# Three row splits and three transposes of a wide unit, moved one unit earlier

## The chip, the cores and the metric

One core of a Trainium2 chip runs the whole kernel. The time is the device time of one execution in microseconds; the number shown for a kernel is the median over several executions.

## The reference

The inputs are q, k and v of 4 batches, 12 heads, 448 positions and 64 columns. The reference computes attention with normalised q and k, and lays the result out as x of 1792 rows and 768 columns. Two mixture layers follow, each with 8 experts:

```
e_idx = argmax(logits of the row)
for e in range(8):
    h = max(x[rows of e] @ w1[e], 0)        # 768 -> 1024
    out[rows of e] = gate[rows of e] * (h @ w2[e])   # 1024 -> 768
```

The first layer has one more gate factor, and the second adds a bias to its logits that depends on a modality number. Each row goes to one expert only, so the rows have to be gathered by expert, multiplied with that expert's two matrices, and scattered back. Everything is in float32.

## The kernel before

**Units.** The work of the two mixture layers is cut into units. A unit is up to 304 rows of one expert: they are gathered from memory into `xr` (three tiles of 128, 128 and 48 rows), multiplied with `w1` (the first product, 8 output blocks, steps 0 to 7) and with `w2` (the second product, 6 output blocks, steps 8 to 13), and scattered to the output. Every float32 operand is split into a float16 high part and a bfloat16 low part, and a product takes three matmuls per pair of 128 by 128 blocks (line 378). The high part is a cast on ScalarE, and the low part a subtraction on VectorE or GpSimd (lines 310 and 311 for weights, 361 and 362 for rows).

**The order of units.** The second layer ends with six units, `seq`: three wide units of up to 304 rows (j = 0, 1, 2), a narrow remainder unit of up to 64 rows (j = 3), a wide unit (j = 4), and a second narrow one (j = 5). The change concerns `seq[4]`, the wide unit between the two remainder units. Below, W2 is `seq[2]`, R3 is `seq[3]`, W4 is `seq[4]`, and R5 is `seq[5]`. A narrow unit has its own planes for rows and for second-layer weights (`XTx`, `wxh`, `wxl`); W2 and W4 share the planes `XT`.

**Preparing a unit's rows.** For a unit, four steps run ahead of its first matmul: its table of rows `pay` is loaded (SyncE, line 345); from this VectorE computes row numbers `idx` (line 352) and GpSimd gathers the rows (line 357); each tile is split (lines 361 and 362) into `XS`; and each tile of `XS` is turned by a DMA transpose into `XT`, issued from SyncE (line 365).

**Where these steps are placed.** `M.unit` calls `do(s)` behind step s. There `XPLAN[late]` gives splits and transposes of the next unit, and `side` gives extra functions by step. `do(0)` also loads `pay` of the unit after the next one, and `do(7)` computes its `idx` and gathers it. Before the change, W2 carries the splits of W4 as `side` functions behind its steps 11, 12 and 13, and R3 carries the three transposes behind its step 1 (`XPLAN[6]`).

**Queues.** Every engine works in the order in which it is given instructions. SyncE issues the weight loads, the loads of `pay`, and the transposes, all on one DMA queue. Around the change its order is: `w1` block 0 and 1 of W4 (tile `r`), then block 2, block 3, block 4 and 5, `pay` of R5, the three transposes, then eight loads of `w2` of W4 (tiles `raw`, `r2a` and `r2b`). The blocks of `r` wait for their six buffers, which the split of R3's `w1` frees one by one. The split of W4's `w1` runs during R3's second product: casts on ScalarE (`w1h`), subtractions on VectorE (`w1l`).

Of the kernel before, what the change touches and what calls it, by code (L numbers as in the profile page):

```python
# [27 lines left out]
class Moe:  # L28
# [366 lines left out]
    def unit(self,u,nx=None,fx=None,side=None,late=0,mid=None,fast={},now=False,fp=0,fr=7,**kw):  # L395

        gen=self.gen(); side=dict(side or {})
        plan=XPLAN[late] if nx is not None else {}
        def do(s):
            if fx is not None and s==fp: self.fetch_pay(fx)  # L400
            for k,t in plan.get(s,()):
                if t<nx.ntl:
                    if k=="t": self.xtrans(nx,t)
                    else: self.xsplit(nx,t,self.nc.gpsimd if k=="p" else None)
            if fx is not None and s==fr: self.fetch_rows(fx)
            for _ in range(fast.get(s,1)): next(gen,None)
            for f in side.pop(s,()): f()
# [90 lines left out]
        yield  # L498
        yield from self.route_g(sp,sm,l,ntl,R,nx["ohsum"],nx["ord"],iv=iv,pay=pay,tag="tp",lag=True)

XPLAN={5:{1:[("s",1),("t",0)],2:[("s",2),("t",1)],3:[("t",2)]},7:{9:[("s",0),("t",0)]},4:{0:[("p",0)],2:[("t",0),("t",1),("t",2)]},6:{1:[("t",0),("t",1),("t",2)]},0:{0:[("p",0),("p",1),("p",2)],7.5:[("t",0),("t",1),("t",2)]},3:{3:[("s",0)],4:[("s",1)],5:[("s",2)],7.5:[("t",0),("t",1),("t",2)]},
1:{8:[("s",0),("s",1),("s",2),("t",0),("t",1),("t",2)]},
    2:{7.5:[("s",0),("s",1),("s",2),("t",0),("t",1),("t",2)]},None:{10:[("s",0),("t",0)]}}
class LazyUnit:
# [329 lines left out]
def body_full(tc,q,k,v,g_q,g_k,wg,wog,w1,w2,mod,wg2,bias2,v1,v2,out,stop=False,O=None):  # L834
    nc=tc.nc
    with ExitStack() as ctx:
        M=Moe(tc,ctx)
# [120 lines left out]
        def stepper(name):  # L958
            def f():
                if name not in S: S[name]=F[name]()  # L960
                next(S[name],None)
            return f
# [18 lines left out]
        sides={1:{KF+j:[stepper("table1")] for j in range(6)},2:{7:[stepper("pick2")]*2,**{j:[stepper("pick2")] for j in range(8,14)}},3:{7:[stepper("pick3")]*2,**{j:[stepper("pick3")] for j in range(8,14)}}}  # L981
# [21 lines left out]
        seq=S["B"][:3]+[S["S"][0],S["B"][3],S["S"][1]]  # L1003
# [8 lines left out]
        def load(t,n): return nc.values_load(t[0:1,0:1],min_val=0,max_val=n)  # L1012
        def chain(n,i,m,unit):
            if i>=m: return
            with tc.If(n>i):
                u=unit(i); cold(u); M.unit(u); M.flush()
                chain(n,i+1,m,unit)
        def others(u,nx,fx):
            def f(done):
                sl,tn=M.slot,M.turn  # L1020
                assert M.post is None
                with tc.If(S["over"]>0):  # L1022
                    ent,ni=S["s1"]
                    chain(load(ni,G1),0,G1,lambda i: Unit(L1,ent,i,128))
                    c=lp.tile([128,E],F32,name="c4"); M.reduce_counts(tp,c2,lp,tag="tp",out=c)
                    rem=lp.tile([128,E],F32,name="rem"); nc.vector.tensor_tensor(out=rem,in0=c,in1=off2,op=ALU.subtract)
                    for _ in M.chunks(S["b4"],lp,M.nchunks(lp,rem,N2,0),off2,c,N2,G4): pass
                    be4,n4=S["b4"]
                    chain(load(n4,G4),0,G4,lambda i: Unit(L2,be4,i,N2))
                    M.redo(u,nx,fx,tn,done)  # L1030
                M.slot,M.turn=sl,tn; u.e=None
                if nx is not None: nx.e=None
            return f
        def known(): S["over"]=load(over,E+G2+G1)
        def px(t): return lambda: M.xsplit(seq[4],t,nc.gpsimd)
        sides={0:{0:[more],3:[known]},2:{KF+3+t:[px(t)] for t in range(3)},4:{KF+1:[nc.gpsimd.drain]}}
        for u in seq: u.own=True
        for j,u in enumerate(seq):
            nx,fx=seq[j+1] if j<5 else None,seq[j+2] if j<4 else None
            M.unit(u,nx=nx,fx=fx,side=sides.get(j),late={2:4,3:6,4:4}.get(j,0),mid=others(u,nx,fx) if j==0 else None)  # L1040
        M.flush()
        pin(tc,mark)

# [28 lines left out]
```

## Time and profile before

| what | value |
|---|---|
| time, median of 3 runs | 881.64 us (878.62 to 884.17) |
| profiled execution | 877.29 us, span 875.6 us |
| mean granted clock of TensorE | 0.98 |
| busy share: TensorE matmul, VectorE, ScalarE, GpSimd | 93%, 74%, 62%, 45% |

The rows below have times in microseconds from the start of the span of the profiled execution. PE is TensorE's matmuls, PEld its weight loads, DVE is VectorE, ACT is ScalarE, POOL is GpSimd and SPq is SyncE's issuing of DMAs. A name such as L365 is the line that issued the instruction, `XT<-XS` says that it writes XT and reads XS. A bracket at a row's end gives how long the engine stood idle before it and what ended that.

### The profile page before, as it was taken

To read this page: it belongs to the slowest core of one execution; us is meant where nothing else is said; L and a number is where in the kernel's file an instruction comes from. 1 tells how busy PE (TensorE), PEld (TensorE's weight loads), DVE (VectorE), ACT (ScalarE), POOL (GpSimd) and SP (SyncE) were. 2 spreads that over 40 slices of the span, in tenths; PEclk is the share of its full clock that TensorE was granted. 3 is DMA by queue.
4 is the path that set the end of the run, shared out by engine and by line. 5 is a ranking of instruction groups with operands and counts; after the bars stand their busy time and mean duration, and the time that the engine had idled before them with its cause. 6 is when DMAs were issued, how large, how long until landed. Compare 5 with 4: busy or idle time off the path is not lost. (4 is left out here: it accounts for less than half of the span.)

```text
span 875.6 us, 23286 instructions
## 1 busy us (share of the span) xinstructions
PE 817.9 (93%) x8881; PEld 640.0 (73%) x8898; DVE 649.3 (74%) x1302; ACT 545.0 (62%) x1039; POOL 389.9 (45%) x397
## 2 busy tenths in 40 slices
PE   4698999998998899899999999999999999999897
PEld 1265666665665588777889999988677768878676
DVE  6689889888778775786797767776676846577674
ACT  4577777776776654655556686776545535456563
POOL 5677777876776623131424333344402524024301
PEclk9799999998999989999999999999999999999999
DMA  5567665766465482979486797898677759896961
GB/s 137 130 152 183 162 155 162 201 161 163 114 172 142 143 229 77 278 290 326 105 321 145 275 320 201 249 348 239 204 251 280 235 108 332 192 315 207 291 245 52
DMA packets 142137, 181.42 MB, mean 207 GB/s; under 512 B 71944, under 2 KB 109592, under 8 KB 142016
## 3 DMA queue, kind: packets, MB, share of 16 engines
q1 hardware_dynamic: 134048, 157.06, 62.9%
q0 software_dynamic: 6656, 22.32, 7.8%
q8 instruction: 71, 1.16, 0.6%
q10 hardware_dynamic: 1312, 0.47, 0.2%
q14 instruction: 50, 0.41, 0.2%
HBM read 129.73 MB, written 23.94 MB: 176 GB/s over the span
## 5 line engine op out<-in xcount | busy, mean ns | idle before, releaser
L378 PE MATMUL pl<-XT,w1h 128*128 128x304 f16 (+6 forms) x1236 | 210.5, 275 | 4.9 <-PEq L1022 2.0
L378 PE MATMUL pl<-hh,w2h 128*128 128x304 f16 (+7 forms) x720 | 194.4, 275 | 0.0
L378 PE MATMUL pl<-hh,w2l 128*128 128x304 f16 (+7 forms) x720 | 194.1, 274 | 0.0
L378 PE MATMUL pl<-hl,w2h 128*128 128x0 bf16 x720 | 187.9, 264 | 3.0 <-DVE hl L382 3.0
L378 PE MATMUL pl<-XT,w1l 128*128 128x304 f16 (+6 forms) x618 | 172.5, 279 | 0.0
L680 POOL TENSOR_TENSOR plo<-p 128x448 f16<-128x448 f32 x142 | 140.3, 1005 | 56.1 <-ACT p L677 52.4
L378 PEld LDWEIGHTS <-w1h 128*128 128x128 f16 x1536 | 134.5, 98 | 27.4 <-ACTq L1022 2.3
L378 PEld LDWEIGHTS <-w2h 128*128 128x128 f16 x1440 | 134.0, 98 | 24.6 <-issue 1.4
L311 DVE TENSOR_TENSOR w1l<-r,w1h 128x1024 bf16<-128x1024 f32 x90 | 109.7, 1233 | 46.5 <-ACT w1h L310 46.5
L456 ACT COPY yt<-pl 128x304 f32<-128x304 f32 (+8 forms) x102 | 36.6, 358 | 117.2 <-PE pl L378 117.2
L362 POOL TENSOR_TENSOR XS<-xr,XS 128x768 bf16<-128x768 f32 (+5 forms) x27 | 46.8, 1749 | 130.4 <-ACT XS L361 100.6
L381 ACT ACTIVATE hh<-pl 128x304 f16<-128x304 f32 (+8 forms) x135 | 49.1, 364 | 81.0 <-PE pl L378 69.5
L677 ACT ACTIVATE p<-pst,eb 128x896 f32<-128x896 f32 (+1 forms) x96 | 86.5, 911 | 14.8 <-PE pst L673 13.9
L310 ACT CAST w1h<-r 128x1024 f16<-128x1024 f32 x90 | 93.5, 1056 | 0.1
L690 PE MATMUL av<-vv,p 128*128 128x65 f16 (+1 forms) x768 | 89.8, 199 | 1.8 <-ACT xrow L702 1.8
L690 PEld LDWEIGHTS <-p 128*128 128x128 bf16 (+1 forms) x768 | 73.5, 102 | 20.8 <-issue 15.0
L692 PE MATMUL av<-vv,plo 128*128 128x65 f16 (+1 forms) x768 | 88.0, 196 | 0.6 <-DVE plo L680 0.6
L691 PE MATMUL av<-vv,p 128*128 128x64 f16 (+1 forms) x768 | 88.5, 198 | 0.0
L654 DVE TENSOR_REDUCE m<-psm 128x2 f16<-128x896 f32 x70 | 76.0, 1086 | 9.1 <-PE psm L649 7.3
L378 PEld LDWEIGHTS <-w1l 128*128 128x128 bf16 x768 | 74.1, 98 | 11.8
L378 PEld LDWEIGHTS <-w2l 128*128 128x128 bf16 x720 | 70.3, 98 | 16.7 <-issue 4.1
L382 DVE SCALAR_TENSOR_TENSOR hl<-pl,hh 128x304 bf16<-128x304 f32 (+8 forms) x135 | 53.5, 398 | 34.8 <-ACT hh L381 34.4
(328 smaller groups left out, 1806.3 us busy)
## 6 DMA issues: line engine op xcount, KB each, us to landing
r<-in_moe_w_dram SPq DMA_DIRECT2D x96, 512.0 KB, 8.9
raw<-in_moe_w_dram SPq DMA_DIRECT2D x64, 384.0 KB, 5.9
r2a<-in_moe_w_dram SPq DMA_DIRECT2D x32, 384.0 KB, 6.8
r2b<-in_moe_w_dram SPq DMA_DIRECT2D x32, 384.0 KB, 8.9
T<-Z SPq DMA_DIRECT2D x48, 224.0 KB, 3.8
T<-Z SPq DMA_DIRECT2D x48, 112.0 KB, 2.9
yd<-zero SPq DMA_DIRECT2D x14, 384.0 KB, 3.1
rv<-in_v_dram SPq DMA_DIRECT2D x24, 192.0 KB, 4.2
```

The lines of the kernel that those rows point to most:

```text
L310: if part!=1: nc.scalar.copy(h,t)
L311: if part!=0: (eng or nc.vector).tensor_tensor(out=l,in0=t,in1=h,op=ALU.subtract)
L362: if part!=0: (eng or nc.vector).tensor_tensor(out=self.XS[:m,t,1].bitcast(BF16),in0=x,in1=h,op=ALU.subtract)
L378: self.nc.tensor.matmul(o,a,b,start=i==0,stop=i==tot-1); i+=1
L381: nc.scalar.activation(h,p,AF.Relu)
L382: nc.vector.scalar_tensor_tensor(out=l,in0=p,scalar=0.0,in1=h,op0=ALU.max,op1=ALU.subtract)
L654: if t<3: nc.vector.tensor_reduce(m[:,t:t+4:3],p[:,:,:S],axis=AX.X,op=ALU.max,negate=True)
L677: self.nc.scalar.activation(self.d["P",i][:,self.u(kt)],p[:,:nn,:S],AF.Exp,bias=self.eb,scale=0.125)
L680: eng.tensor_tensor(out=self.d["L",i][:,u],in0=P[:,u],in1=self.hi(P)[:,u],op=ALU.subtract)
L690: nc.tensor.matmul(o,hh,w[:,0:65],start=kt==0,stop=False)
L691: nc.tensor.matmul(o[:,0:64],hh,w[:,65:129],start=False,stop=False)
L692: nc.tensor.matmul(o,ll,w[:,0:65],start=False,stop=kt==3)
```

## The change

The splits of W4's rows move from behind steps 11, 12 and 13 of W2 to behind its steps 10, 11 and 12. The transposes move from behind step 1 of R3 to behind steps 11, 12 and 13 of W2, each one step behind its split. R3's plan for its next unit is then empty (`XPLAN[8]`).

```
-6:{1:[("t",0),("t",1),("t",2)]}
+8:{}
...
         def px(t): return lambda: M.xsplit(seq[4],t,nc.gpsimd)
-        sides={0:{0:[more],3:[known]},2:{KF+3+t:[px(t)] for t in range(3)},4:{KF+1:[nc.gpsimd.drain]}}
+        def tx(t): return lambda: M.xtrans(seq[4],t)
+        sides={0:{0:[more],3:[known]},2:{KF+2:[px(0)],KF+3:[px(1),tx(0)],KF+4:[px(2),tx(1)],KF+5:[tx(2)]},4:{KF+1:[nc.gpsimd.drain]}}
...
-            M.unit(u,nx=nx,fx=fx,side=sides.get(j),late={2:4,3:6,4:4}.get(j,0),mid=others(u,nx,fx) if j==0 else None)
+            M.unit(u,nx=nx,fx=fx,side=sides.get(j),late={2:4,3:8,4:4}.get(j,0),mid=others(u,nx,fx) if j==0 else None)
```

KF is 8. The loads of W4's `w1` blocks are issued inside the same steps of W2, ahead of the `side` functions: blocks 0 and 1 in step 11, block 2 in step 12, block 3 in step 13, blocks 4 and 5 behind it. So SyncE's new order is: blocks 0 and 1, transpose 0, block 2, transpose 1, block 3, transpose 2, blocks 4 and 5, `pay` of R5, the eight loads of `w2`.

## Rows read from the trace of the kernel before

**Rows 1.** The page: busy time, share of the span, instructions of each engine.
```profile
PE 817.9 (93%) x8881; PEld 640.0 (73%) x8898; DVE 649.3 (74%) x1302; ACT 545.0 (62%) x1039; POOL 389.9 (45%) x397
```

**Rows 2.** The chain that ended last, 803 to 847: start, us, what.
```profile
803.22 2.08 POOL XS L362
...
806.59 1.73 POOL XS L362
...
808.71 1.66 POOL XS L362
...
813.14 6.96 DMA XT<-XS
...
820.14 3.92 PE pl L378 x18
...
824.17 22.33 PE pl L378 x174
```

**Rows 3.** TensorE in order of time, 817.9 to 820.2.
```profile
817.93 0.30 PE L444 MATMUL pty<-ident,yt 128*128 128x128 f32 x1 [0.37 <-DVE yr L447]
820.14 0.43 PE L378 MATMUL pl<-XT,w1h 128*128 128x304 f16 x1 [1.92 <-DMA XT<-XS]
```

**Rows 4.** One stretch: PE, PEld, DVE, ACT, POOL busy; then granted clock, DMA share, GB/s.
```profile
820.14:824.10 3.96, 3.96 (x20) 2.59 (x21) 2.60 (x5) 1.56 (x2) 0.76 (x1) 0.62 1.04 397
```

**Rows 5.** ScalarE in order of time, 800 to 818.
```profile
800.31 0.41 ACT L456 COPY yt<-pl 128x304 f32<-128x304 f32 x1 [1.34 <-PE pl L378]
...
802.29 0.83 ACT L361 CAST XS<-xr 128x768 f16<-128x768 f32 x1
...
817.16 1.09 ACT L310 CAST w1h<-r 128x1024 f16<-128x1024 f32 x1
```

**Rows 6.** SyncE's DMA issues in order of time, 792 to 816; us is the issuing.
```profile
792.99 13.74 SPq L317 DMA_DIRECT2D r<-in_moe_w_dram  x6
...
806.41 0.33 SPq L317 DMA_DIRECT2D r<-in_moe_w_dram  x1
807.53 0.55 SPq L345 DMA_DIRECT2D pay<-o  x1
808.19 1.34 SPq L365 DMA_TRANSPOSE XT<-XS  x1
809.64 3.41 SPq L365 DMA_TRANSPOSE XT<-XS  x1
813.14 2.75 SPq L365 DMA_TRANSPOSE XT<-XS  x1
```

**Rows 7.** DMA issues: xcount, KB, median us to landing; two stretches, then the page.
```profile
r<-in_moe_w_dram SPq DMA_DIRECT2D x6, 512.0 KB, 5.3
...
XT<-XS SPq DMA_TRANSPOSE x3, 8.9
...
r<-in_moe_w_dram SPq DMA_DIRECT2D x96, 512.0 KB, 8.9
pay<-o SPq DMA_DIRECT2D x9, 4.0 KB, 8.7
```

**Rows 8.** VectorE in order of time, 811.7 to 821.6.
```profile
811.97 0.16 DVE L352 TENSOR_TENSOR idx<-pay,iv 128x1 int32<-128x1 f32 x1
812.05 0.23 DVE L382 SCALAR_TENSOR_TENSOR hl<-pl,hh 128x64 bf16<-128x64 f32 x1
812.99 2.36 DVE L311 TENSOR_TENSOR w1l<-r,w1h 128x1024 bf16<-128x1024 f32 x2 [0.71 <-ACT w1h L310]
816.16 0.29 DVE L447 TENSOR_TENSOR yr<-pty,pay 128x128 f32<-128x128 f32 x1 [0.81 <-DMA out_dram<-yr,idx]
...
820.37 1.22 DVE L311 TENSOR_TENSOR w1l<-r,w1h 128x1024 bf16<-128x1024 f32 x1
```

**Rows 9.** The gather of W4's rows: POOL in order of time, then its DMAs' landing.
```profile
792.02 1.77 POOL L357 DMA_INDIRECT xr<-yd,idx  x1 [0.30 <-issue]
...
xr<-yd,idx POOLq DMA_INDIRECT x3, 5.9
```

More of the change, by code (lines that the diff above doesn't have):

```diff
@@ L499, in route2 @@
         yield from self.route_g(sp,sm,l,ntl,R,nx["ohsum"],nx["ord"],iv=iv,pay=pay,tag="tp",lag=True)
-XPLAN={5:{1:[("s",1),("t",0)],2:[("s",2),("t",1)],3:[("t",2)]},7:{9:[("s",0),("t",0)]},4:{0:[("p",0)],2:[("t",0),("t",1),("t",2)]},6:{1:[("t",0),("t",1),("t",2)]},0:{0:[("p",0),("p",1),("p",2)],7.5:[("t",0),("t",1),("t",2)]},3:{3:[("s",0)],4:[("s",1)],5:[("s",2)],7.5:[("t",0),("t",1),("t",2)]},
+XPLAN={5:{1:[("s",1),("t",0)],2:[("s",2),("t",1)],3:[("t",2)]},7:{9:[("s",0),("t",0)]},4:{0:[("p",0)],2:[("t",0),("t",1),("t",2)]},8:{},0:{0:[("p",0),("p",1),("p",2)],7.5:[("t",0),("t",1),("t",2)]},3:{3:[("s",0)],4:[("s",1)],5:[("s",2)],7.5:[("t",0),("t",1),("t",2)]},
 1:{8:[("s",0),("s",1),("s",2),("t",0),("t",1),("t",2)]},
```

## Prediction

> **What bounds the kernel now.** I read the page's busy shares first: TensorE's matmuls fill 93% of the span [rows 1], so a change of order can only win TensorE's idle time, or its time at a lower clock. Then the chain of work that ended last, around the moved steps. Up to the narrow unit R3 the chain runs over matmuls; there it leaves TensorE and goes through W4's rows: subtraction on GpSimd, issue on SyncE, transpose on the DMA engines, and back to TensorE at 820.14 [rows 2]. Third, TensorE in order of time: it has its last instruction of R3 at 817.93 and then stands idle for 1.92 us until a transpose lands [rows 3]. Fourth, the granted clock: W4's first block, behind that idle time, runs at 0.62 on average, a mix of the levels 2.4 and 1.2 GHz [rows 4]. The target of the change is thus real, and small: 1.92 us of waiting, and the slow block. To tell whether it is won I read the engines that the moved steps pass through [rows 5 to 9].
>
> **Splits.** Nothing is added; three casts and three subtractions come one step sooner. The cast for tile 0 would stand where ScalarE is idle today, in the 1.34 us before the copy at 800.31, so from 798.97 on; a row cast takes 0.83 us and fits [rows 5], so its cost is nothing. If that idle time were gone it would delay one copy by at most 0.83 us. The rows must be there: the last gather was issued at 792.02 and lands 5.9 us later, at 797.9 [rows 9], 1.1 us before the first cast. The subtractions then end at about 799.8 + 2.08 = 801.9 for tile 0; tile 1 takes tile 0's old place and ends at 803.22 + 2.08 = 805.3; tile 2 takes tile 1's place and, with its own 1.66 us, ends at 806.59 + 1.66 = 808.25 [rows 2]. It was 810.37.
>
> **Transposes and SyncE's queue.** This is where the change costs. SyncE issued six blocks `r` in 13.74 us from 792.99 on [rows 6], each as its buffer came free. Now transpose 0 stands behind the first two blocks and waits for the split until 801.9. With 1.34 us per issue [rows 6] the order becomes: transpose 0 at 801.9, block 2 at 803.3, transpose 1 at 805.3, block 3 at 806.7, transpose 2 at 808.3, block 4 at 809.7, block 5 at 810.1. Block 5 was issued at 806.41. The load of `pay` for R5 followed it by 807.53 - 806.41 = 1.12 us [rows 6]; it now goes out at 811.2, which is 3.7 us later. The eight loads of W4's `w2` go out behind it, from about 811.8 on; today they wait for the last transpose's issue, until 813.14 + 2.75 = 815.9 [rows 6]. They come sooner, and as TensorE waits for none of them I count nothing.
>
> The last transpose, issued at 808.3, lands after 6.96 us (the same tile before [rows 2]) to 8.9 us (the middle one of the three [rows 7]); I take its own row, 815.3. TensorE wants it at 818.2, and 817.2 would do as well. So the 1.92 us wait for XT is gone.
>
> The late blocks: block 5 is issued at 810.1 and lands after 5.3 us (median of these six) or 8.9 us (median of all 96) [rows 7], at 815.4 to 819.0. ScalarE casts it at 817.16 [rows 5]. At 815.4 this costs nothing. At 819.0 the cast is 1.8 us late, and the subtraction behind it ends at 819.0 + 1.09 + 1.22 = 821.3, still under the 820.37 + 1.22 = 821.59 at which VectorE's own row of work ends today [rows 8]. VectorE's backlog covers it.
>
> **What is late next, without any new wait.** A full-clock matmul of a wide unit takes 22.33 / 174 = 0.128 us of the chain [rows 2]. If W4 starts at 817.93 + 0.30 = 818.2 [rows 3], its last of six weight blocks has its turn 15 matmuls later, at 820.1. But `w1l` of that block ends at 821.59 [rows 8]. Three more matmuls, 0.5 us with the last one's drain, end the first output block at 822.1. It ended at 820.14 + 3.92 = 824.06 [rows 2], as its 18 matmuls took 3.92 us in place of 2.3. So wait and slow clock together give back **-1.9 us**, not 1.92 + 1.6; the rest is capped by VectorE.
>
> **The new wait.** VectorE computes `idx` of R5 from `pay` at 811.97 today, without waiting [rows 8]. Behind it in VectorE's order stand `hl` of R3's last block (812.05), which R3's second product on TensorE needs, and then all six `w1l` subtractions of W4. GpSimd's gather of R5 waits for `idx` too. If `pay` lands at time P, VectorE stands from 811.97 to P. Its chain has slack: 0.71 us idle before `w1l` 0, and 0.81 us idle for the scatter of W2 [rows 8], which GpSimd can now begin sooner because its last subtraction ends 2.1 us earlier. Together 1.52 us. W4's first block shifts by P - 811.97 - 1.52.
>
> No row gives this `pay`'s landing. Before, it was there 811.97 - 807.53 = 4.4 us after its issue, or sooner. The bounds from rows: not before its issue, 811.2, which is no stall at all; and 8.7 us, the median of the 4 KB loads of `pay` [rows 7], which is 819.9, a stall of 7.9 and a shift of 6.4. As the queue has block 5 ahead of it, I take the nearest row, the six `r` blocks: 810.1 + 5.3 = **P = 815.4**. The stall is 3.4 us, the shift 3.4 - 1.5 = **+1.9 us**. The Trainium skill, page "SBUF — State Buffer", section "The DMA setup-cost knee", puts a transfer at about 2 us fixed plus bytes over 436 GB/s; by that estimate 1 KB lands at 813.2, and the sum would be -1.9 instead of 0. No row here shows that landing by itself.
>
> **Sum.** -1.9 + 1.9 = 0.0, so 877.3 us for the profiled execution. That one lies 4.35 us under the median of the runs, 881.64; a median of the changed kernel is then **881.6 us**. With the bounds: at the low end no stall, and the scatter's 0.81 us saved as well, -2.7; at the high end -1.9 + 6.4 = +4.5.
>
> One thing is left open in size. The 1.92 us that TensorE stood idle were followed by the lower clock, which cost 3.92 - 2.3 = 1.6 us [rows 2, 4]. The stall on `hl` would move such a stretch from W4 into R3's second product, whose pace ScalarE's casts set, so I count 0 for it, and 1.6 as its bound.
>
> **The rivals.** *Forecast, the trade*: wait for XT gone, wait for `pay` in its place, between -1 and +1, 881.6 us, chance 0.41.
>
> *The full gain*: `pay` overtakes the blocks, or these land fast, so that P is at or below 811.97 + 1.52 = 813.5, 2.3 us after its issue. For it: the load is tiny. Against it: two 512 KB blocks ahead on the same queue, issued 1.5 and 1.1 us before. Gain 1.9 to 2.7, some 879.3 us. The rule of the page named above would have it so. Chance 0.24.
>
> *Slower*: P passes 815.4 by over 1 us. Its place is SyncE: with two transposes in the queue, issuing took 3.41 and 2.75 us in place of 1.34 [rows 6]. That adds 2.07 + 1.41 = 3.5 us to the 811.2, so `pay` goes out at 814.7, and with the 4.4 us that it had at most today P is 819.1. Then the stall is 7.1, the shift 5.6, the net +3.7: 885.3 us. It decides from P = 815.4 on. For it: W2's scatter moves at this time. Against: here the transposes are spaced by 3 us. Chance 0.28.
>
> *The change doesn't bring XT sooner*: transpose 2 waits behind transpose 1 in the queue, 3.5 us of issuing and then 8.9 us to landing, 820.7 [rows 6, 7]; then the 1.92 us wait stays, the `w1l` shift hides in the slow first block, and the time is that of before, 881.6 us. Chance 0.07.
>
> **How the numbers follow.** The runs of before spread by 2.5 to 3.0 us about their median, and the terms from -2.7 to +4.5. The range leaves out the tails of both: 877.5 to 886. One per cent, 8.8 us, is about what a measurement of this kernel can tell from no change; no case reaches it, in either direction. Faster 0.01, within 0.97, slower 0.02 (a longer stall and a slow clock on top).
>
> **What would show it.** Right: no row of TensorE in W4 that waits for XT; VectorE idle for about 3 us before `idx` of R5, put down to the DMA of `pay`; TensorE idle in R3's second product, waiting for `hl`; the `r` blocks 2 to 5 issued 4 to 7 us later, between the transposes. Wrong: `idx` without a wait and W4 starting at 818 (the full gain); a `pay` landing past 817 (slower); or a wait of ScalarE for `r` during the casts of `w1h`, which I counted as covered.

## Result: slower by 0.6%

| | kernel before | changed kernel |
|---|---|---|
| median of 22 runs each | 879.71 us | 884.48 us |
| ratio, 95% interval | | 1.0063 (1.0045 to 1.0081) |
| profiled span | 875.6 us | 883.9 us |
| R3's first matmul starts at | 807.2 us | 810.7 us |
| from there to the end of the span | 68.4 us | 73.2 us |

The two profiled spans differ by 8.3 us, but 3.4 us of this arise ahead of R3, in work that the change does not touch: W2's first product already starts that much later. Over the profiles of this study R3 starts between 803 and 814 us. From R3 on the changed kernel takes 4.9 us longer (73.24 against 68.36), which agrees with the ratio (0.0063 x 880 = 5.5 us, with an interval from 4.0 to 7.1 us). Below, a time written R3+x counts from R3's first matmul of the same profile.

The chain of the changed kernel, in order of time (start, us, what), from SyncE's last block `r` to W4's first output block:

```profile
814.57 0.34 SPq L317
...
815.74 7.08 DMA pay<-o
...
822.92 0.13 DVE idx L352
823.05 0.18 DVE hl L382
...
824.84 1.07 PE pl L378 x24
825.91 0.27 PE pty L444
...
828.73 0.67 PE pl L378 x24
...
829.98 2.47 PE pl L378 x18
```

XT is gone from the chain, and `pay` stands where the three subtractions and the transpose stood [rows 2]. W4's first 18 matmuls take 2.47 us in place of 3.92 us. VectorE says the same, idle time in the bracket:

```profile
815.17 0.20 DVE L351 TENSOR_SCALAR iv<-pos,s2gc 128x1 f32<-128x1 f32 x1
822.92 0.16 DVE L352 TENSOR_TENSOR idx<-pay,iv 128x1 int32<-128x1 f32 x1 [7.54 <-DMA pay<-o]
823.00 0.22 DVE L382 SCALAR_TENSOR_TENSOR hl<-pl,hh 128x64 bf16<-128x64 f32 x1
823.13 1.22 DVE L311 TENSOR_TENSOR w1l<-r,w1h 128x1024 bf16<-128x1024 f32 x1
```

Before, `idx` waited for nothing [rows 8]. Now it waits 7.54 us, and `hl` of R3's last block and all of `w1l` stand behind it. SyncE's issues show why `pay` is late:

```profile
805.32 1.47 SPq L365 DMA_TRANSPOSE XT<-XS  x1
807.03 0.71 SPq L317 DMA_DIRECT2D r<-in_moe_w_dram  x1
808.77 2.20 SPq L365 DMA_TRANSPOSE XT<-XS  x1
811.21 0.71 SPq L317 DMA_DIRECT2D r<-in_moe_w_dram  x1
812.23 1.20 SPq L365 DMA_TRANSPOSE XT<-XS  x1
813.67 0.65 SPq L317 DMA_DIRECT2D r<-in_moe_w_dram  x1
814.57 0.34 SPq L317 DMA_DIRECT2D r<-in_moe_w_dram  x1
815.74 0.55 SPq L345 DMA_DIRECT2D pay<-o  x1
```

Transposes and blocks alternate, and `pay` goes out at R3+5.1, where it was R3+0.3 [rows 6]. It then takes 7.08 us to land.

The stretches of the changed kernel, with columns as in [rows 4], show what it does to TensorE:

```profile
814.20:823.27 9.07, 1.71 (x59) 1.57 (x56) 0.87 (x6) 1.56 (x4) 1.58 (x2) 0.72 1.10 327
823.27:829.50 6.23, 6.23 (x127) 5.88 (x126) 5.84 (x8) 5.33 (x10) 1.34 (x1) 0.58 1.03 380
```

TensorE is busy for 1.71 of the first 9.07 us; it waits 7.4 us for `hl`. R3's second product, in the second stretch, then runs at a granted clock of 0.58 on average: 0.50, the level of 1.2 GHz, in most of it, and 1.00 from 828.73 on.

### The profile page after: what moved, and what is told of

It reads as the page before. It is cut to its first block, busy times and chain, and to the rows that moved or that the text cites. A ratio compares the mean times of both kernels' runs of the same rounds, so it can differ in the third digit from the quotient of the medians.

```text
span 883.9 us, 23285 instructions
## 1 busy us (share of the span) xinstructions
PE 821.2 (93%) x8881; PEld 642.7 (73%) x8898; DVE 648.7 (73%) x1302; ACT 546.1 (62%) x1039; POOL 390.1 (44%) x397
## 5 line engine op out<-in xcount | busy, mean ns | idle before, releaser
L378 PE MATMUL pl<-XT,w1h 128*128 128x304 f16 (+6 forms) x1236 | 207.7, 273 | 2.7 <-PEq L1022 2.0
L690 PEld LDWEIGHTS <-p 128*128 128x128 bf16 (+1 forms) x768 | 74.2, 103 | 21.1 <-issue 15.3
```

The costliest lines, as they stand in the source:

```text
L378: self.nc.tensor.matmul(o,a,b,start=i==0,stop=i==tot-1); i+=1
L690: nc.tensor.matmul(o,hh,w[:,0:65],start=kt==0,stop=False)
```

## The experiments

Theory A: the loss is VectorE standing for `pay`. Rivals: B, W4's late `w1` blocks hold it by themselves; C, XT is still late; D, the earlier splits cost by their place. E came up on the way: W2's scatter and W4's transposes collide on the DMA engines. F: `pay`'s landing time is its queue alone.

| kernel | R3's first matmul to the end, us | ratio to before, 95% |
|---|---|---|
| before | 68.4 | |
| changed | 73.2 | 1.0063 (1.0045 to 1.0081) |
| e1_pay_early | 66.9 | 1.0000 (0.9975 to 1.0025) |
| e7_before_pay_early | 65.7 | 0.9968 (0.9938 to 0.9997) |
| e3_splits_alone | 72.0 | 1.0052 (1.0028 to 1.0077) |
| e6_pay_early_pool | 68.5 | 0.9985 (0.9957 to 1.0012) |
| e8_splits_scatter_held | 68.1 | 1.0002 (0.9981 to 1.0023) |
| e9_after_scatter_held | 72.9 | 1.0074 (1.0045 to 1.0103) |
| e10_pay_early_scatter_held | 69.8 | 1.0051 (1.0022 to 1.0079) |
| e12_pay_act_timed | 65.6 | 0.9969 (0.9944 to 0.9994) |
| e11_splits_held_pay_early | 65.4 | 0.9956 (0.9931 to 0.9982) |

The middle column is one profile each. It and the ratio agree to 1.0 us, but for e1, e6, e9 and e10, where they are 1.5, 1.5, 2.0 and 3.1 us apart; for these the ratio counts.

**e1: `pay` ahead of everything, else the changed kernel.**

```
-2:{KF+2:[px(0)], ...
+2:{KF:[lambda: M.fetch_pay(seq[5])],KF+2:[px(0)], ...
-            M.unit(u, ...
+            M.unit(u, ... fp=99 if j==3 else 0, ...     # no load of pay in R3
```

> The changed kernel with one difference: the load of pay for R5 is issued in W2 behind its step 8, ahead of W4's six w1 blocks and the three transposes, in place of behind them. All numbers count from R3's first matmul, where W4's first output block ends at 16.8 us in the kernel before and 21.8 us in the changed one. Theory A (the whole loss is VectorE standing before idx for pay): idx does not wait, R3's second product is unbroken, W4's first block ends at about 14.9 us, the time is 1.9 us under before (ratio 0.998) and some 7 us under the changed kernel. Rival B (the late w1 blocks 4 and 5, which landed at 10.2 and 11.9 us, hold W4 by themselves): ScalarE's casts of w1h wait for r, W4's first block ends at 16.5 us or later, ratio 1.000 or more. Rival C (transposes sooner do not matter at all, W4 waits for XT again): a wait for XT of 1 us or more.

The loss is gone: 6.3 us less than the changed kernel from R3 on, and a ratio of 1.000. VectorE in e1:

```profile
815.02 0.16 DVE L352 TENSOR_TENSOR idx<-pay,iv 128x1 int32<-128x1 f32 x1
```

No wait, so A holds for the loss. W4's first block ends at R3+15.3, not at the 14.9 of theory A, and rival B has its part in that. ScalarE in e1, and below it block 5 in the chain of e1:

```profile
822.91 1.04 ACT L310 CAST w1h<-r 128x1024 f16<-128x1024 f32 x1 [1.65 <-DMA r<-in_moe_w_dram]
```

```profile
814.10 8.73 DMA r<-in_moe_w_dram
```

The last cast waits 1.65 us for block 5, which takes 8.73 us from its issue. XT was not waited for, so C falls.

**e7: the control, `pay` early in the kernel before.** The edit is that of e1, on the kernel before.

> The kernel before with the load of pay for R5 moved to behind step 8 of W2; splits and transposes where they were. It is the control of e1. Theory A: pay was not waited for in the kernel before, so nothing changes: W4's first block ends at 16.8 us from R3's first matmul (16.3 to 17.3), W4 waits for XT about 1.9 us, ratio 1.000. If pay's place does something by itself (a transpose that comes 0.6 us sooner because pay is out of its way): 0.5 us less. Rival B says the same here.

The expectation missed. Nobody waited for `pay`, and yet moving it gained 2.7 us from R3 on. With it out of the way the first transpose is issued at R3-0.4, not R3+0.95, and the wait for XT falls from 1.9 to 0.7 us. W4's slow first block goes too: its 18 matmuls take 2.98 us at a granted clock of 1.00, not 3.92 us at 0.62. These two make 2.2 of the 2.7 us. From the waits of e7 (who, for whom: us, times, longest):

```profile
PE pl L378 <- DMA XT<-XS: 0.7, 1, 0.7
```

**e3: the splits sooner, the transposes where they were.**

```
-2:{KF+3+t:[px(t)] for t in range(3)}
+2:{KF+2+t:[px(t)] for t in range(3)}
```

> Half of the change: W4's splits behind steps 10 to 12 of W2, the transposes still behind step 1 of R3 and so behind the w1 blocks and pay. Theory A (the move of the transposes in SyncE's order is what costs): no wait of idx for pay, no slower than before; the last transpose lands 0 to 2 us sooner, as it is held by the two transposes ahead of it and not only by its split, so W4's first block ends at 15.3 to 16.8 us from R3's first matmul, ratio 0.998 to 1.000. Rival D (the earlier splits, on ScalarE and GpSimd in W2, cost by themselves): W2's second product longer, or ratio over 1.003.

Slower by 0.5%, which theory A did not foresee. GpSimd in e3, and below it the chain of e3:

```profile
808.75 2.20 POOL L362 TENSOR_TENSOR XS<-xr,XS 48x768 bf16<-48x768 f32 x1 [1.25 <-ACT XS L361]
811.31 1.02 POOL L387 DMA_INDIRECT out_dram<-yr,idx  x1 [0.36 <-DVE hl L382]
```

```profile
811.84 4.31 SPq L365
...
816.24 8.36 DMA XT<-XS
...
824.65 4.71 PE pl L378 x18
```

R3 starts at 809.4 here. GpSimd is done with W4's splits sooner, and its next work, W2's scatter, begins at R3+1.9 in place of R3+3.3. The second transpose now holds SyncE for 4.31 us (3.41 before [rows 6]), and the third lands after 8.36 us (6.96 before [rows 2]). TensorE's wait for XT grows from 1.9 to 4.8 us.

**e8: e3 with the scatter held back** until behind step 3 of R3.

```
+            M.unit(u, ... fast={0:0,1:0,2:0} if j==3 else {}, ...
```

> e3 (W4's splits one step sooner, transposes where they were) with W2's last transpose on TensorE and its scatter held back from behind R3's step 0 to behind its step 3, which puts the scatter's first issue at about 3.4 us from R3's first matmul, where the kernel before had it (3.3), in place of 1.9. Theory E (the earlier splits free GpSimd sooner, W2's three scatters then collide on the DMA engines with W4's transposes 1 and 2): the last transpose lands at 12.9 us or sooner, as before, against 15.2 in e3; W4's first block ends at 16.0 to 17.0 us; ratio 0.998 to 1.001, against 1.005. Rival D (the splits cost by their place on ScalarE or GpSimd, whatever the scatter does): the transposes land at 15 us again, ratio 1.004 or more.

The scatter begins at R3+3.4. The last two transposes, in the chain of e8:

```profile
814.73 3.28 SPq L365
...
818.11 6.60 DMA XT<-XS
```

The second holds SyncE for 3.28 in place of 4.31 us, the third lands after 6.60 in place of 8.36 us, and the ratio is 1.000. D falls and E stands. The edit also moves W2's last transpose on TensorE and its `yr`; neither is in e8's chain.

**e9: the changed kernel with the scatter held.** The edit is that of e8.

> The changed kernel with W2's scatter held back in the same way, to about 3.4 us from R3's first matmul; pay stays behind the blocks and transposes. It tells what pay's 7.1 us from issue to landing were. Theory E (the scatter on the DMA engines): block 3, transpose 2, blocks 4 and 5 and pay land ahead of most of the scatter, pay within 5.5 us of its issue, idx waits 5.5 us or less in place of 7.5, ratio 1.002 to 1.004. Rival F (the queue alone: two blocks and a transpose ahead of pay, whatever the scatter does): 7 us again, ratio 1.006.

`pay` in the chain of e9, and VectorE behind it:

```profile
817.20 6.99 DMA pay<-o
```

```profile
824.28 0.16 DVE L352 TENSOR_TENSOR idx<-pay,iv 128x1 int32<-128x1 f32 x1 [7.26 <-DMA pay<-o]
```

6.99 against 7.08 us: the scatter's start at R3+1.9 is not what delays `pay`. E's forecast missed, and F's number came. That the queue alone does it is not shown, as the held scatter still runs while `pay` is under way. What the traces do show, by the completions of DMAs recorded in them, is an order: `pay` lands right behind block 5 of `r`. Block 5 landed 3.6 us after its issue in the kernel before, 3.5 in e3, 8.0 in the changed kernel and 7.1 in e9. The changed kernel differs from e3 in the place of the transposes alone, so that move is what made block 5, and `pay` behind it, late.

**e5 and e12: `pay` from ScalarE's queue**, the same step of the program, else the changed kernel.

```
-        if rem: nc.sync.dma_start(...
+        if rem: (q or nc.sync).dma_start(...     # q=nc.scalar for j==3
```

> The changed kernel with the load of pay for R5 issued from ScalarE's own DMA queue, at the same step of the program (behind R3's step 0), not from SyncE's. It asks what the load costs when it stands behind nothing on its queue while the same DMA engines are busy. Theory A with the setup rule of the notes: issued at about 1 us from R3's first matmul, landing 2 to 3 us later, so idx does not wait. Theory E: the engines are shared, landing takes 4 us or more, idx waits up to 1 us. In both, R3's second product is unbroken and W4's first block ends under 16.5 us, against 21.8 in the changed kernel; rival B: 16.5 or more, as the w1 blocks 4 and 5 are late.

> e5 again, the changed kernel with pay on ScalarE's own queue, now timed, since e5 was a single run that began R3 at 803.5 us, 3.8 us ahead of the kernel before, which is nothing of pay's. Theory A: R3's first matmul to the end is 67 to 68 us (e5 67.6, before 68.3), no wait of idx over 0.5 us, ratio 0.998 to 1.001. If e5's time was pay's doing: ratio 0.994 or less.

e5 was a single run of 872.79 us, and `idx` waited 0.3 us in it, as theory E said. Timed, the kernel stands at 878.43 against 881.20 us. From R3 on e12 takes 65.6 us, less than the 67 to 68 that were expected, and its ratio of 0.997 lies between the two branches of the expectation. ScalarE's queue and VectorE in e12:

```profile
806.90 0.60 ACTq L345 DMA_DIRECT2D pay<-o  x1
```

```profile
811.43 0.16 DVE L352 TENSOR_TENSOR idx<-pay,iv 128x1 int32<-128x1 f32 x1 [0.49 <-DMA pay<-o]
```

With no other load ahead of it on ScalarE's queue, `pay` still takes about 811.4 - 806.9 = 4.5 us. It goes out 4.2 us sooner after R3's start than in the changed kernel, ahead of the third transpose and of blocks 4 and 5, and so `idx` waits 0.49 in place of 7.54 us. This is a second way to take the loss away, and it bears out theory A. It does not tell what the other queue is worth by itself: by the completions, `pay` lands here 0.2 us behind block 3, the last block issued ahead of it on any queue, so on SyncE's own queue it might have landed as soon. Block 5 still takes 7.85 us in the chain of e12.

**e6: e1 with two of the six `w1l` on GpSimd.**

```
-            if warm and not nx.px: self.warm2(db,None,soon)
+            if warm and not nx.px: self.warm2(db,nc.gpsimd if soon else None,soon)
```

> e1 plus one edit: in R3, the low parts of w1 blocks 1 and 3 of W4 are subtracted on GpSimd in place of VectorE. It tests the step of the prediction that without any wait W4's first block is capped by VectorE's chain of six subtractions. If that cap is real: W4's first block ends at 13.6 to 14.4 us from R3's first matmul, against 14.9 in e1, ratio 0.997. If it is not (the w1 blocks land too late, rival B, or GpSimd's subtraction of over 2 us is itself late): no sooner than e1.

No sooner than e1: W4's first block ends at R3+16.7, against 15.3. The blocks `r` came too late for the cap to be tested here, as the waits of e6 show:

```profile
ACT w1h L310 <- DMA r<-in_moe_w_dram: 3.1, 2, 1.8
```

**e10: e1 with the scatter held.** The edits are those of e1 and e8.

> e1 (the changed kernel with pay ahead of everything) with W2's scatter held back to about 3.4 us from R3's first matmul. In e1 ScalarE's casts waited 1.7 us for w1 blocks that landed at 9.8 and 12.6 us. Theory E: these blocks land 1.5 us or more sooner, the casts wait under 0.5 us, W4's first block ends at 14.5 to 15.2 us against 15.7, ratio 0.996 to 0.998. Against it: VectorE's first yr of R3 has to wait for the scatter, which now ends later, 0.5 to 2 us; then no better than e1.

The caution in the last sentence came true. The waits of e10:

```profile
DVE yr L447 <- DMA out_dram<-yr,idx: 3.3, 1, 3.3
```

VectorE may not overwrite `yr` until W2's scatter has read it, and the held scatter ends too late for it. The casts, too, still waited 1.5 us for a block `r`, so theory E's step failed as well: 0.5% slower than before.

**e11: what the runs point to.** e8 and `pay` early.

> The version that the runs so far point to: e8 (W4's splits one step sooner, transposes behind R3's step 1 as before, W2's scatter held to behind R3's step 3) and pay for R5 ahead of W4's w1 blocks, as in e1 and e7. So no transpose stands ahead of a w1 block or of pay, and the scatter begins at 3.4 us from R3's first matmul. Theory E with A: transposes go out from -0.4 us on, the last lands at 10 to 11.5 us (e8 12.4, e7 10.7), the wait for XT is under 0.5 us, no wait for pay or for r, R3's first matmul to the end of the kernel is 65.5 to 67 us (before 68.3, changed 73.2, e7 65.7), ratio 0.996 to 0.999. If e7's gain was chance or pay's place does nothing with the scatter held: 68 us and ratio 1.000, as e8.

The expectation came, at the good end of its ranges, and this is the lowest ratio of all: 876.51 against 881.20 us. Its chain has neither `pay` nor XT in it:

```profile
816.37 1.21 DVE w1l L311
...
820.61 1.13 DVE w1l L311
...
823.13 0.30 PE pl L378
```

It now goes over VectorE's subtractions of W4's `w1`. Its interval overlaps those of e7 and e12, so it is not shown to be better than these.

## Why the prediction was wrong

The forecast was a trade that comes out even, 881.6 us. The range held the measured median, but the kernel became slower, the way of the third rival. Step by step:

- **The wait for XT goes**: right. W4's matmuls have no wait for it, and its slow first block went with it.
- **A new wait of VectorE for `pay`, with `hl`, TensorE and `w1l` behind it**: right in place and order.
- **P = 815.4, the step that failed.** The prediction had `pay` issued at R3+4.0 and landing at R3+8.2. It was issued at R3+5.1 and landed at R3+12.2. Of these 4.0 us, 1.1 are the issue. The third split took 2.20 us, not the 1.66 us of its row before, so the third transpose went out 0.5 us late. Block 5 went out 0.9 us behind block 4, not 0.4, as SyncE waited 0.6 us for VectorE's `hl`. The other 2.9 us are the landing, 7.08 us against 4.2. That `pay` lands with the last of the `r` blocks was right: block 5 landed at R3+11.9, right ahead of it. The size of that block's landing was wrong: 8.0 us, not 5.3. The 5.3 came from six blocks on a queue without transposes between them. The 8.9 us that the prediction named for the same block as its other bound, or the 8.7 us of the other `pay` loads [rows 7], were nearer.
- **Shift = stall - 1.52, less 1.9**: with the measured P it gives 12.2 - 4.7 - 1.5 - 1.9 = +4.1 us; W4's first block ended 4.9 us later. What makes the 0.8 us left is not shown. The low clock, which the prediction counted as 0 with a bound of 1.6, is one candidate: R3's groups of 24 matmuls took 1.07 us at a clock of 0.50 and 0.67 at 1.00. But with the transpose between them, 0.27 us, their pace was 1.34 us, and VectorE's pair of a `w1l` and a `yr` took 1.33 us in both kernels. From the last `hl` to R3's last matmul it was 6.3 us, against 6.0 before.
- **The late `w1` blocks are covered by VectorE**: not tested in the changed kernel, where the stall hid them, and wrong where it is taken away: ScalarE waits 1.65 us for them in e1.
- **The splits cost nothing**: right for their place on ScalarE and GpSimd (e8: 1.000 with the same splits), wrong for what follows. With the transposes in their old place they cost 0.5% (e3), through the scatter that starts sooner. The prediction booked that start as slack for VectorE and named it in favour of the slower rival, but gave no price for what the scatter would meet on the DMA engines. In the changed kernel itself, holding the scatter back gained nothing (e9).
- **VectorE's `w1l` is late next**: borne out by the chain of e11.
- **The rule on a transfer's fixed 2 us** (the Trainium skill, "SBUF — State Buffer", "The DMA setup-cost knee"): it would have `pay` land within the full gain. The trace disagrees: 7.1 us in the queue, and 4.5 us on a queue of its own while other transfers run.

The rival that came true named SyncE's stretched issuing as the cause and +3.7 us as the price. Its place and direction were right. That its P, R3+11.9, is so close to the measured R3+12.2 is luck: it had the issue at R3+7.5, 2.4 us too late, and the landing at 4.4 us, 2.7 us too short.

## What to carry to other kernels

When a step moves up in an in-order DMA queue, list everything that it now stands ahead of, down to the smallest load, and who waits for that: here 1 KB of row numbers held VectorE for 7.5 us while 1.9 us of waiting were saved. An engine that is freed sooner starts its next work sooner; if that is a DMA, ask what it meets. Here the small load could go first: that alone, on the kernel before, gained 2.7 us from R3 on (e7), more than the 1.9 us that the whole change was after.

## What had not been expected of the hardware

Indirect writes that begin 1.5 us sooner, in the middle of three DMA transposes, lengthen the last transpose's landing from 6.6 (e8) to 8.4 us (e3) and its neighbour's issuing from 3.3 to 4.3 us. A load of 512 KB that was issued among transposes took 8.0 us to land, against 3.6 us in the kernel before; whether the transposes ahead of it or the scatter that ran at that time did it was not separated. A load of 1 KB took 4.5 us with no other load ahead of it on its queue, while the DMA engines were at work for other queues. What share of this is the engines and what the load's own fixed time was not measured.
